# One rotation of three PSUM banks for the first product, the transposes and x, in place of one bank and a rotation of two

## The chip, the cores and the metric

The kernel runs on one core of one Trainium2 chip. The metric is the device time of one execution in microseconds (us), median of several runs. TensorE (PE in the rows), VectorE (DVE), ScalarE (ACT), GpSimd (POOL) and SyncE (SP, which issues the DMAs) each have a queue of their own that runs strictly in its order, and wait for each other through semaphores.

## The reference

Windowed attention with four sink tokens, then a gated MLP (the code calls it MoE; there is one expert). Batch 4, 8 heads, 768 positions, head size 64, window 128; the model is 512 wide, the hidden layer 1024. In short:

```python
scores = scale * np.matmul(q, k.transpose(0, 1, 3, 2))
scores = np.where(is_sink | in_window, scores, -1000000000.0)
a = softmax(scores)                         # in float32
x = np.matmul(a, v) .transpose(0, 2, 1, 3).reshape(B, S, H * D)
h = np.maximum(x @ w_in, 0.0)
conv_out[s] = sum(conv_w[k] * h[s + k - 1] for k in range(3))
gate = 1.0 / (1.0 + np.exp(-conv_out))
return h * gate @ w_out
```

## The kernel before

**Attention.** Heads are taken in pairs; pair `g` (0 to 15, four to a batch) has six query tiles of 128 rows, `t` = 0 to 5. `prep`/`prep32` turn q and k on TensorE (tiles `trq`, `trk` for batch 0, `tq`, `tk` after it), `scores` makes a tile of scores (`sc`, L330 in batch 0, L333 and L334 later), DVE takes the window and the maximum (L509, L510), ACT the exponential (L513), POOL scales by the sum (L518), `transp` turns the result (`pts`, L534 and L548), `transp_sinks` turns the sinks (`tk`, L541 and L568), and `pv` multiplies by v into `px` (L586, L609). `xout` copies `px` into the model's x, split into a high part `xH` (ACT, L341) and a low part `xL` (DVE, L342). For batch 0 `pv` works on half pairs, later on a whole pair, and then it holds two `px` tiles at once. Batch 0 is worked as pairs 0 to 3, first half, then pairs 0 to 3, second half.

**The MLP.** It is cut into 96 units: unit `n` has 256 positions and 128 hidden columns, 24 units to a batch. `first` makes the first product in 12 matmuls into `ph` (L184: each of four slices of the model takes three products, xH by wiH, xH by wiL, xL by wiH). `gate` reads `ph` once (ACT, L191), and then does the convolution and the gate: ACT L195, DVE L196 and L197, ACT L198, DVE L199, POOL L201 and L202, which write `g`. `second` multiplies `g` into `po` with six matmuls of 512 columns (L211). `pieces` lists these steps, the second product of a unit two units behind its first (`TRAIL` is 2), and `banded` hands them out between the steps of the attention at an even rate. A batch's units need the whole x of that batch, so units 24 to 47 come after `px` of pair 7; in batch 0 the `px` of pair 3's first half completes the first 384 positions, and units 0 to 7 (positions 0 to 255) can begin with them.

**The order.** The program text gives an order, but the Tile framework's scheduler then moves instructions: by its own estimate of times it puts on each engine's queue whatever it holds to be ready, within what data and buffers allow. `c.pin` does nothing in this version. A PSUM tile with a tag is put into the banks of that tag in turn, in the order of the program text: with `bufs=3`, a tile can't be written before the readers of the third one ahead of it are done. Eight banks are in use: `sc` 2, `pts` 1, `po` 2, and in the kernel before `h` 1 (the tiles `ph`) and `T` 2 (all turned tiles and `px`).

**Weights.** w_in and w_out come as 64-bit floats; `narrow` makes 32-bit ones on ACT (L112) and DVE (L113, L114, L115), and ACT and POOL split them (L122, L123). This goes on beside the attention of batch 0.

Of the kernel before, what the change touches and what calls it, by code (L numbers as in the profile page):

```python
# [10 lines left out]
F32 = mybir.dt.float32  # L11
F32R = mybir.dt.float32r
# [5 lines left out]
P = 128  # L18
# [43 lines left out]
class Moe:  # L62
# [62 lines left out]
    def taps(self, raw):  # L125
        c, nc = self.c, self.c.nc
        w = self.narrow(raw)
        pt = self.ps.tile([P, 512], F32, tag="T", name="cwt", bufs=2)
        c.pin(nc.tensor.transpose(pt[:, 0:3 * self.NFF], w, c.ident[0:3 * self.NFF, 0:3 * self.NFF]))
        nc.scalar.copy(self.cw.rearrange("p k f -> p (k f)"), pt[:, 0:3 * self.NFF])  # L130

# [31 lines left out]
    def unit(self, n):  # L163

        c, nc, mp = self.c, self.c.nc, self.mp
        NFF = self.NFF
        bc, ff = divmod(n, NFF)
        b, ch = divmod(bc, self.NCH)
        xH, xL = self.x(b)
        wH, wL = self.wi  # L170
        t0, t1 = max(0, CH * ch - 2), min(c.S, CH * ch + CH + 2)
        W = t1 - t0
        d0 = 1 if t1 < c.S else 3
        o = d0 - 1 + CH * ch - t0
        prods = [(w, x, cc) for cc in range(self.NCC) for (w, x) in ((wH, xH), (wL, xH), (wH, xL))]
        u = Ctx()

        def first(lo):
            if lo == 0:
                self.need(max(self.place[f"wi{ff * P // 512}_{self.NCC - 1}"], self.place["taps"]) + 1)  # L180
                u.h = self.ps.tile([P, 512], F32, tag="h", name=f"ph{n}")
            for i in range(lo, lo + 4):
                w, x, cc = prods[i]
                c.pin(nc.tensor.matmul(u.h[:, 0:W], w[:, cc, ff * P:(ff + 1) * P], x[:, cc, t0:t1],  # L184
                                       start=(i == 0), stop=(i == len(prods) - 1)))
            if lo + 4 == len(prods):
                gate()

        def gate():
            hb, cw = self.hb[n % 2], self.cw  # L190
            nc.scalar.activation(hb[:, d0:d0 + W], u.h[:, 0:W], AF.Relu, scale=0.5)  # L191
            prev, this, nxt = (hb[:, o + i:o + i + CH] for i in range(3))
            a = mp.tile([P, CH], F32, tag="t1", name=f"t1{n}")
            e = mp.tile([P, CH], F32, tag="t2", name=f"t2{n}")
            nc.scalar.mul(a, prev, cw[:, 0, ff:ff + 1])  # L195
            nc.vector.scalar_tensor_tensor(out=e, in0=this, scalar=cw[:, 1, ff:ff + 1], in1=a, op0=ALU.mult, op1=ALU.add)  # L196
            nc.vector.scalar_tensor_tensor(out=a, in0=nxt, scalar=cw[:, 2, ff:ff + 1], in1=e, op0=ALU.mult, op1=ALU.add)  # L197
            nc.scalar.activation(e, a, AF.Tanh)  # L198
            nc.vector.scalar_tensor_tensor(out=a, in0=e, scalar=1.0, in1=this, op0=ALU.add, op1=ALU.mult)  # L199
            u.g = mp.tile([P, 2, CH], F32R, tag="g", name=f"g{n}", bufs=NGB)  # L200
            nc.gpsimd.tensor_scalar(u.g[:, 0], a, 1.0, 1.0, ALU.mult, ALU.mult)  # L201
            nc.gpsimd.tensor_tensor(out=u.g[:, 1], in0=a, in1=f(u.g[:, 0]), op=ALU.subtract)  # L202

        def second(tt):
            self.need(self.place[f"wo{ff}"] + 1)
            if ff == 0:
                self.po[tt] = self.ps.tile([P, 512], F32, tag="po", name=f"po{n}{tt}", bufs=NT)
            po = self.po[tt]
            oH, oL = self.wo
            for i, (a, w) in enumerate(((0, oH), (0, oL), (1, oH))):  # L210
                c.pin(nc.tensor.matmul(po[:, 0:c.DM], u.g[:, a, tt * P:(tt + 1) * P], w[:, ff, :],  # L211
                                       start=(ff == 0 and i == 0), stop=(ff == NFF - 1 and i == 2)))
            if ff == NFF - 1:
                st = self.temp("st", c.DM, 3)
                nc.scalar.copy(st, po[:, 0:c.DM])
                nc.sync.dma_start(c.out[b, ch * CH + tt * P:ch * CH + (tt + 1) * P, :], st)

        u.first = [lambda lo=lo: first(lo) for lo in range(0, len(prods), 4)]
        u.second = [lambda tt=tt: second(tt) for tt in range(NT)]
        return u  # L220
# [15 lines left out]
class Attn:  # L236
# [15 lines left out]
    def prep(self, g, s, ahead=lambda: None):  # L252
# [4 lines left out]
        s.plain = False  # L257

        def turn_q(half):
            pt = self.mps.tile([P, HTL, P], F32, tag="T", name=f"tq{g}{half}", bufs=2)  # L260
            for t in range(HTL):
                c.pin(nc.tensor.transpose(pt[:, t, :], s.raw["q", half][:, t].rearrange("p a d -> p (a d)"), c.ident))  # L262
            ahead()
            X = s.X[half] = ap.tile([P, 2, HTL, P], F32R, tag="X", name=f"X{g}{half}", bufs=3)
            rows = [slice(D * j, D * j + D) for j in range(2)]
            for j in range(2):
                self.evac(X[rows[j], j], pt[rows[j]], -1.0 / math.sqrt(D))
            c.emptied = [nc.vector.scalar_tensor_tensor(out=X[rows[1 - j], j], in0=pt[rows[j]], scalar=-1.0 / math.sqrt(D),
                                                        in1=f(X[rows[j], j]), op0=ALU.mult, op1=ALU.subtract) for j in range(2)]

        def turn_k(half):
            if half == 0:
                if g % 2 not in self.KK:
                    self.KK[g % 2] = ap.tile([P, 4, T, kw], F32R, tag="kk", name=f"kk{g}")
                    for j in range(2):
                        r = slice(D - D * j, P - D * j)
                        plane = f(self.KK[g % 2][r, 2 + j]).rearrange("p t k -> p (t k)")
                        if self.zeros is None:
                            nc.gpsimd.memset(plane, 0.0)
                        else:  # L280
                            nc.sync.dma_start(plane, self.zeros[r])
                s.kk = self.KK[g % 2]
            kk = s.kk[:, :, HTL * half:HTL * half + HTL, 0:P]
            pt = self.mps.tile([P, HTL, P], F32, tag="T", name=f"tk{g}{half}", bufs=2)
            for t in range(HTL):
                c.pin(nc.tensor.transpose(pt[:, t, :], s.raw["k", half][:, t].rearrange("p a d -> p (a d)"), c.ident))
            ahead()
            for j in range(2):
                nc.scalar.copy(kk[:, j], pt)
            rows = [slice(D * j, D * j + D) for j in range(2)]  # L290
            c.emptied = [nc.vector.tensor_tensor(out=kk[r, 2 + j], in0=pt[r], in1=f(kk[r, j]), op=ALU.subtract)
                         for j, r in enumerate(rows)]
            if half == 0 and kw > P:
                nc.scalar.copy(s.kk[:, :, :, P:kw], f(s.kk[:, :, 0:1, 0:kw - P]).to_broadcast([P, 4, T, kw - P]))
            if half:
                nc.sync.dma_start(f(s.kk[D:P, 0]), f(s.kk[0:D, 0]))
                nc.sync.dma_start(f(s.kk[0:D, 1]), f(s.kk[D:P, 1]))
# [3 lines left out]
    def prep32(self, g, half, s, kk, tag, ahead):  # L301
# [2 lines left out]
        tiles = slice(HTL * half, HTL * half + HTL)  # L304

        def turn(nm):
            pt = self.mps.tile([P, HTL, P], F32, tag=tag, name=f"tr{nm}{g}{half}", bufs=2)
            for t in range(HTL):
                c.pin(nc.tensor.transpose(pt[:, t, :], s.raw[nm, half][:, t].rearrange("p a d -> p (a d)"), c.ident))
            if nm == "q":  # L310
# [79 lines left out]
def banded(c):  # L390
# [136 lines left out]
    def transp(g, t):  # L527
        s = st[g]
        hf, u = divmod(t, 3)
        if g < NPAIR:  # L530
# [4 lines left out]
            s.pT[t] = ap.tile([P, 2, 2, P], F32, tag="pT", name=f"pT{g}_{t}", bufs=PTB)  # L535
            nc.scalar.copy(s.pT[t][:, 0:parts], pts[:, 0:parts])  # L536
            if u == 2:
                pk = m.ps.tile([P, P], F32, tag="T", name=f"tk{g}_{t}", bufs=2)
                sk = ap.tile([P, 6, SP], F32, tag="sk", name=f"sk{g}_{hf}")
                nc.scalar.copy(sk, s.pe[hf].rearrange("p t h k -> p (t h) k")[:, :, P:P + SP])  # L540
                c.pin(nc.tensor.transpose(pk[0:6 * SP, :], sk.rearrange("p t k -> p (t k)"), c.ident))  # L541
# [20 lines left out]
    def transp_sinks(g, t):  # L562
        s = st[g]
        hf, u = divmod(t, 3)
        if g < NPAIR or u < 2:
            return
        pk = m.ps.tile([P, P], F32R, tag="T", name=f"tk{g}_{t}", bufs=2)
        c.pin(nc.tensor.transpose(pk[0:3 * SR, :], s.sk.rearrange("p a t k -> p (a t k)"), c.identr))  # L568
        s.sT[hf] = ap.tile([3 * SR, P], F32R, tag="sT", name=f"sT{g}_{hf}")
        s.cut.append(nc.scalar.copy(s.sT[hf], f(pk[0:3 * SR, :])))  # L570
# [1 line left out]
    def pv(g, t):  # L572
# [4 lines left out]
        if u < 2 or (g >= NPAIR and hf == 0):  # L577
            return
        halves = [hf] if g < NPAIR else [1, 0]
        px = {h: m.ps.tile([P, 3, P], F32, tag="T", name=f"px{g}_{h}", bufs=2).rearrange("p t k -> p (t k)") for h in halves}  # L580
        open_ = set()

        def product(j, kt, qt, pT):
# [30 lines left out]
    def prep(n):  # L614

        g, half = jobs[n]
        if g >= NPAIR and half:
            return []
        if g >= PLAIN:
            return A.prep(g, st[g], ahead)  # L620
        out = []
        for h in (half, half + 1)[0:1 + g // NPAIR]:
            out += A.prep32(g, h, st[g], kks[g // 2][:, g % 2], "po" if g < NPAIR and h == 0 else "T", ahead)
        return out

    def values(n):
# [83 lines left out]
def general(c):  # L710
# [12 lines left out]
    for g in range(c.B * NPAIR):  # L723
# [7 lines left out]
        for t in range(T):  # L731
            u = t % 3
            if u == 0:
                px = m.ps.tile([P, 3, P], F32, tag="T", name=f"px{g}_{t}", bufs=2)
            keep = gp.tile([P, S], F32, tag="keep", name=f"keep{g}_{t}", bufs=1)
            tmp = gp.tile([P, S], F32, tag="tmp", name=f"tmp{g}_{t}", bufs=1)
            wt = gp.tile([P, 1], F32, tag="wt", name=f"wt{g}_{t}", bufs=1)
# [112 lines left out]
```

## Time and profile before

| what | value |
|---|---|
| median of 3 runs | 501.5 us (501.25 to 502.39) |
| the profiled execution | 502.03 us |
| its span, first to last instruction | 499.9 us |
| TensorE busy | 458.4 us (92%) |
| VectorE, ScalarE, GpSimd busy | 359.9, 344.1, 287.6 us |
| mean granted TensorE clock | 0.98 of full speed |

The profiled execution's time is 2.13 us more than its span, and 0.53 us more than the median of the runs. A busy share is over the whole span; the rows below split it by stretch.

### The profile page before, as it was taken

What the parts mean: (1) busy time and instruction counts of PE and PEld (TensorE: products, weight loads), DVE (VectorE), ACT (ScalarE), POOL (GpSimd) and SP (SyncE); (2) the same over time, 40 slices, a digit from 0 to 9 for tenths busy, and PEclk for the clock granted to TensorE, in tenths of its full rate; (3) what the DMA queues carried; (4) which work ended last, traced back from release to release, by engine and by line L of the source; (5) the groups of instructions that cost most, each with busy time, mean ns of one, the idle gap of its engine ahead of it and who ended that gap; (6) DMA issues with size and microseconds to landing.
All of it is one profiled execution on the core that took longest, in us unless ns stands there. A gap on an engine that the chain in (4) does not pass through costs nothing.

```text
span 499.9 us, 10494 instructions
## 1 busy us (share of the span) xinstructions
PE 458.4 (92%) x3181; PEld 395.6 (79%) x3181; DVE 359.9 (72%) x1212; ACT 344.1 (69%) x1066; POOL 287.6 (58%) x558
## 2 busy tenths in 40 slices
PE   2878889998999999789999999999999999999993
PEld 1656678877888898578888898988888887889892
DVE  4677999767968787787876968596868663555561
ACT  3987897778858776685876777685967654444542
POOL 3457586643775656546674757475647673444441
PEclk9987899999999999899999999999999999999998
DMA  5875762246232423316241242143220100101101
GB/s 146 216 197 166 204 200 49 57 108 161 66 82 67 111 65 94 102 24 145 48 122 45 55 120 52 23 114 73 70 70 2 43 2 8 36 1 42 42 4 50
DMA packets 87307, 41.03 MB, mean 82 GB/s; under 512 B 80160, under 2 KB 80184, under 8 KB 87240
## 3 DMA queue, kind: packets, MB, share of 16 engines
q1 hardware_dynamic: 87240, 40.25, 30.9%
q8 instruction: 28, 0.46, 0.4%
q14 instruction: 39, 0.32, 0.2%
HBM read 27.60 MB, written 6.29 MB: 68 GB/s over the span
## 4 chain that ended last, share of the span: by engine, by line
PE 62%; DVE 14%; ACT 10%; POOL 5%; issue 3%; DMA 3%; SPq 2%; POOLq 0%; DVEq 0%; ACTq 0%
PE po L211 20%; PE ph L184 19%; PE px L586 7%; DVE t L197 3%; PE sc L333 3%; PE sc L334 3%; PE pts L548 3%; DVE t L196 2%; PE px L609 2%; PE sc L330 2%; ACT t L195 2%; ACT hb L191 2%; ACT t L198 1%; PE tq L262 1%; DVE stm L114 1%
## 5 line engine op out<-in xcount | busy, mean ns | idle before, releaser
L211 PE MATMUL po<-woH,g 128*128 128x512 f32 x384 | 139.4, 407 | 4.0 <-POOL g L201 3.9
L184 PE MATMUL ph<-xH,wiH 128*128 128x258 f32 (+1 forms) x384 | 111.9, 292 | 6.2 <-ACT hb L191 4.2
L184 PE MATMUL ph<-xL,wiH 128*128 128x258 f32 (+1 forms) x384 | 110.0, 286 | 0.4 <-DVE xL L342 0.4
L184 PE MATMUL ph<-xH,wiL 128*128 128x258 f32 (+1 forms) x384 | 108.9, 284 | 0.0
L201 POOL TENSOR_SCALAR g<-t 128x256 fp32r<-128x256 f32 x96 | 42.3, 441 | 75.2 <-DVE t L199 59.7
L211 PEld LDWEIGHTS po<-woH,g 128*128 128x128 f32 x384 | 70.0, 188 | 16.6 <-POOL g L201 5.7
L184 PEld LDWEIGHTS ph<-xH,wiH 128*128 128x128 f32 x384 | 72.7, 189 | 12.1 <-ACT hb L191 6.4
L202 POOL TENSOR_TENSOR g<-t,g 128x256 fp32r<-128x256 f32 x96 | 77.9, 812 | 5.4
L518 POOL TENSOR_SCALAR pe<-pe,sm 128x132 f32<-128x132 f32 (+1 forms) x144 | 62.3, 444 | 30.3 <-DVE sm L516 19.4
L211 PE MATMUL po<-woL,g 128*128 128x512 f32 x192 | 76.4, 398 | 0.0
L196 DVE SCALAR_TENSOR_TENSOR t<-hb,cw,t 128x256 f32<-128x256 f32 x96 | 51.2, 533 | 34.9 <-ACT t L195 34.7
L184 PEld LDWEIGHTS ph<-xH,wiL 128*128 128x128 f32 x384 | 72.7, 189 | 2.5
L184 PEld LDWEIGHTS ph<-xL,wiH 128*128 128x128 f32 x384 | 72.8, 190 | 1.9 <-DVE xL L342 1.4
L198 ACT ACTIVATE t<-t 128x256 f32<-128x256 f32 x96 | 40.1, 417 | 46.8 <-DVE t L197 46.4
L513 ACT ACTIVATE pe<-pe,sm 128x132 f32<-128x132 f32 (+1 forms) x144 | 58.0, 404 | 19.2 <-DVE sm L510 18.2
L199 DVE SCALAR_TENSOR_TENSOR t<-t,hb 128x256 f32<-128x256 f32 x96 | 45.4, 473 | 20.2 <-ACT t L198 19.5
L197 DVE SCALAR_TENSOR_TENSOR t<-hb,cw,t 128x256 f32<-128x256 f32 x96 | 54.8, 570 | 5.4
L195 ACT ACTIVATE t<-hb,cw 128x256 f32<-128x256 f32 x96 | 49.1, 511 | 5.6 <-POOL g L202 1.4
L191 ACT ACTIVATE hb<-ph 128x258 f32<-128x258 f32 (+1 forms) x96 | 36.9, 385 | 20.8 <-PE ph L184 20.2
L552 POOL TENSOR_SCALAR_AFFINE_SELECT pT<-pT 128x256 f32<-128x256 f32 x60 | 27.2, 454 | 40.1 <-ACT pT L550 32.4
L333 PE MATMUL sc<-kk,X 128*128 128x260 f32 (+1 forms) x144 | 44.1, 316 | 4.6 <-DVE sm L510 3.9
L586 PE MATMUL px<-pT,vraw 128*64 128x128 f32 (+1 forms) x512 | 44.6, 327 | 2.7 <-ACT pT L536 2.3
(145 smaller groups left out, 963.0 us busy)
## 6 DMA issues: line engine op xcount, KB each, us to landing
raw<-in_q_dram SPq DMA_DIRECT2D x64, 96.0 KB
raw<-in_k_dram SPq DMA_DIRECT2D x64, 96.0 KB
out_dram<-stm SPq DMA_DIRECT2D x24, 256.0 KB
kk<-kk SPq DMA_DIRECT2D x24, 198.0 KB
vraw<-in_v_dram SPq DMA_DIRECT2D x24, 192.0 KB
wi_0r<-in_moe_w_in_dram SPq DMA_DIRECT2D x2, 512.0 KB
wi_1r<-in_moe_w_in_dram SPq DMA_DIRECT2D x2, 512.0 KB
wi_2r<-in_moe_w_in_dram SPq DMA_DIRECT2D x2, 512.0 KB
```

The source lines that it names most:

```text
L184: c.pin(nc.tensor.matmul(u.h[:, 0:W], w[:, cc, ff * P:(ff + 1) * P], x[:, cc, t0:t1], start=(i == 0), stop=(i == len(prods) - 1)))
L191: nc.scalar.activation(hb[:, d0:d0 + W], u.h[:, 0:W], AF.Relu, scale=0.5)
L195: nc.scalar.mul(a, prev, cw[:, 0, ff:ff + 1])
L196: nc.vector.scalar_tensor_tensor(out=e, in0=this, scalar=cw[:, 1, ff:ff + 1], in1=a, op0=ALU.mult, op1=ALU.add)
L197: nc.vector.scalar_tensor_tensor(out=a, in0=nxt, scalar=cw[:, 2, ff:ff + 1], in1=e, op0=ALU.mult, op1=ALU.add)
L199: nc.vector.scalar_tensor_tensor(out=a, in0=e, scalar=1.0, in1=this, op0=ALU.add, op1=ALU.mult)
L202: nc.gpsimd.tensor_tensor(out=u.g[:, 1], in0=a, in1=f(u.g[:, 0]), op=ALU.subtract)
L211: c.pin(nc.tensor.matmul(po[:, 0:c.DM], u.g[:, a, tt * P:(tt + 1) * P], w[:, ff, :], start=(ff == 0 and i == 0), stop=(ff == NFF - 1 and i ...
L333: self.c.pin(self.nc.tensor.matmul(pc, X[:, j, u, :], kk[:, j, lo:hi], start=True, stop=False))
L513: nc.scalar.activation(pe[:, j, cols], pe[:, j, cols], AF.Exp, bias=sm[:, j:j + 1], scale=-1.0, accum_out=sm[:, 2 + 2 * j:3 + 2 * j])
L518: nc.gpsimd.tensor_scalar(pe[:, j, cols], pe[:, j, cols], sm[:, 8 + j:9 + j], 1.0, ALU.mult, ALU.mult)
L586: ins = nc.tensor.matmul(px[h][D * j:D * j + D, P * at:P * at + n], s.v[:, kt, j, :], pT, start=(h not in open_), stop=False, skip_group_c ...
```

## The change

The tiles `ph` and all tiles of the old tag `T` get one tag, `h`, with three buffers. The number of banks in use stays eight, and no instruction is added or taken away: each engine has the same work. What differs is the order in which tiles take a bank, and with it the order that the scheduler gives to every engine.

```diff
@@ taps, unit
-        pt = self.ps.tile([P, 512], F32, tag="T", name="cwt", bufs=2)
+        pt = self.ps.tile([P, 512], F32, tag="h", name="cwt", bufs=3)
...
-                u.h = self.ps.tile([P, 512], F32, tag="h", name=f"ph{n}")
+                u.h = self.ps.tile([P, 512], F32, tag="h", name=f"ph{n}", bufs=3)
@@ prep, prep32
-            pt = self.mps.tile([P, HTL, P], F32, tag="T", name=f"tq{g}{half}", bufs=2)
+            pt = self.mps.tile([P, HTL, P], F32, tag="h", name=f"tq{g}{half}", bufs=3)
...
-            pt = self.mps.tile([P, HTL, P], F32, tag=tag, name=f"tr{nm}{g}{half}", bufs=2)
+            pt = self.mps.tile([P, HTL, P], F32, tag=tag, name=f"tr{nm}{g}{half}", bufs=3 if tag == "h" else 2)
@@ banded: transp, transp_sinks, pv, prep
-                pk = m.ps.tile([P, P], F32, tag="T", name=f"tk{g}_{t}", bufs=2)
+                pk = m.ps.tile([P, P], F32, tag="h", name=f"tk{g}_{t}", bufs=3)
...
-        px = {h: m.ps.tile([P, 3, P], F32, tag="T", name=f"px{g}_{h}", bufs=2).rearrange("p t k -> p (t k)") for h in halves}
+        px = {h: m.ps.tile([P, 3, P], F32, tag="h", name=f"px{g}_{h}", bufs=3).rearrange("p t k -> p (t k)") for h in halves}
...
-            out += A.prep32(g, h, st[g], kks[g // 2][:, g % 2], "po" if g < NPAIR and h == 0 else "T", ahead)
+            out += A.prep32(g, h, st[g], kks[g // 2][:, g % 2], "po" if g < NPAIR and h == 0 else "h", ahead)
```

(Left out: the same edit for `tk` in `prep` and `transp_sinks`, and for `px` in `general`, the branch that these inputs don't take.)

TensorE's queue, pairs 7 and 8, just ahead of pair 7's `px`, in the kernel before. In a name the number behind the kind is the pair or the unit, then comes the query tile; the last number is a running one.

```order
L262 MATMUL tq81_2656<-ident_85,raw3_70 128x128 x3
L286 MATMUL tk90_2752<-ident_85,raw0_67 128x128 x3
L333 MATMUL sc8_0_0_2703<-kk4_1145,X80_2601 128x128
L334 MATMUL sc8_0_0_2703<-kk4_1145,X80_2601 128x128
L333 MATMUL sc8_0_1_2704<-kk4_1145,X80_2601 128x128
L334 MATMUL sc8_0_1_2704<-kk4_1145,X80_2601 128x128
L548 MATMUL pts_177<-ident_85,pe7_1_2560 128x128
L333 MATMUL sc8_1_0_2763<-kk4_1145,X80_2601 128x260
L334 MATMUL sc8_1_0_2763<-kk4_1145,X80_2601 128x260
L548 MATMUL pts_177<-ident_85,pe7_1_2560 128x128
L333 MATMUL sc8_1_1_2764<-kk4_1145,X80_2601 128x260
L334 MATMUL sc8_1_1_2764<-kk4_1145,X80_2601 128x260
```

The same place, from the scores of pair 8's first tile on, in the changed kernel:

```order
L211 MATMUL po160_2393<-woH_111,g20_2555 128x512
L211 MATMUL po160_2393<-woL_112,g20_2555 128x512
L211 MATMUL po161_2397<-woH_111,g20_2555 128x512
L211 MATMUL po161_2397<-woL_112,g20_2555 128x512
L333 MATMUL sc8_0_0_2703<-kk4_1145,X80_2601 128x128
L334 MATMUL sc8_0_0_2703<-kk4_1145,X80_2601 128x128
L548 MATMUL pts_177<-ident_85,pe7_1_2560 128x128 x2
L211 MATMUL po160_2393<-woH_111,g20_2555 128x512
L211 MATMUL po161_2397<-woH_111,g20_2555 128x512
L333 MATMUL sc8_0_1_2704<-kk4_1145,X80_2601 128x128
L334 MATMUL sc8_0_1_2704<-kk4_1145,X80_2601 128x128
L184 MATMUL ph23_2747<-xH0_116,wiH_109 128x258
```

In the kernel before no matmul of a unit stands between these scores; its next one, of unit 24, comes behind `px` of pair 7. In the changed kernel units 20 to 23 stand here. Counted over the whole queue, this many units' first products are complete ahead of each `px` (a fraction is a unit in work), and this many second products:

| ahead of `px` of pair | 4 | 5 | 6 | 7 | 8 | 9 | 11 | 15 |
|---|---|---|---|---|---|---|---|---|
| first products, before | 14 | 19 | 24 | 24.75 | 28 | 35 | 47 | 72 |
| first products, changed | 13 | 17 | 20 | 24 | 30 | 37 | 48 | 72 |
| second products, before | 11.67 | 16 | 21 | 24 | 26 | 32 | 44 | 69 |
| second products, changed | 10.67 | 15.67 | 19.67 | 23 | 28.67 | 35 | 47 | 70.67 |

TensorE's queue early in batch 0, in the kernel before, and then the same place in the changed kernel:

```order
L330 MATMUL sc2_2_1_513<-kks1_158,X20_322 128x260
L330 MATMUL sc3_0_0_541<-kks1_158,X30_446 128x128
L184 MATMUL ph0_736<-xH0_116,wiH_109 128x258
L184 MATMUL ph0_736<-xH0_116,wiL_110 128x258
L330 MATMUL sc3_0_1_542<-kks1_158,X30_446 128x128
L184 MATMUL ph0_736<-xL0_117,wiH_109 128x258
L330 MATMUL sc3_1_0_582<-kks1_158,X30_446 128x260
L534 MATMUL pts_177<-ident_85,roomL_119 128x128 x4
```

```order
L330 MATMUL sc2_2_1_513<-kks1_158,X20_322 128x260
L330 MATMUL sc3_0_0_541<-kks1_158,X30_446 128x128
L330 MATMUL sc3_0_1_542<-kks1_158,X30_446 128x128
L330 MATMUL sc3_1_0_582<-kks1_158,X30_446 128x260
L534 MATMUL pts_177<-ident_85,roomL_119 128x128 x4
```

Unit 0's matmuls stood one or two at a time between the attention's; now the first of them stands at this place, behind `px` of pair 3's first half:

```order
L586 MATMUL px3_0_721<-pT3_0_596,vraw1_72 64x128 x2
L609 MATMUL px3_0_721<-sT3_0_684,kks1_158 128x128 x2
L184 MATMUL ph0_736<-xH0_116,wiH_109 128x258
L184 MATMUL ph0_736<-xH0_116,wiL_110 128x258
L184 MATMUL ph0_736<-xL0_117,wiH_109 128x258
L184 MATMUL ph0_736<-xH0_116,wiH_109 128x258
L309 MATMUL trk11_741<-ident_85,raw3_70 128x128 x3
```

VectorE's queue when the scores of pair 0's fourth tile arrive (L510, `sc0_3`), in the kernel before, and then in the changed kernel; `stm` are the weights being narrowed, three instructions to a slice:

```order
L114 SCALAR_TENSOR_TENSOR stm21_624<-wi1_0r_580,stm21_624 128x512
L342 TENSOR_TENSOR xL0_117<-px2_0_598,xH0_116 128x384
L115 SCALAR_TENSOR_TENSOR stm21_624<-stm22_625,stm21_624 128x512
L510 ISA roomH_118,sm2_165<-sc0_3_0_662,roomH_118 128x260
L510 ISA sm2_165 128x1
L510 ISA roomH_118,sm2_165<-sc0_3_1_663,roomH_118 128x260
L510 ISA sm2_165 128x1
L113 TENSOR_SCALAR stm23_652<-stm24_653 128x512
L114 SCALAR_TENSOR_TENSOR stm23_652<-wi1_1r_632,stm23_652 128x512
```

```order
L114 SCALAR_TENSOR_TENSOR stm21_624<-wi1_0r_580,stm21_624 128x512
L115 SCALAR_TENSOR_TENSOR stm21_624<-stm22_625,stm21_624 128x512
L342 TENSOR_TENSOR xL0_117<-px2_0_598,xH0_116 128x384
L113 TENSOR_SCALAR stm23_652<-stm24_653 128x512
L114 SCALAR_TENSOR_TENSOR stm23_652<-wi1_1r_632,stm23_652 128x512
L115 SCALAR_TENSOR_TENSOR stm23_652<-stm24_653,stm23_652 128x512
L510 ISA roomH_118,sm2_165<-sc0_3_0_662,roomH_118 128x260
L510 ISA sm2_165 128x1
L510 ISA roomH_118,sm2_165<-sc0_3_1_663,roomH_118 128x260
```

The slice wi1_1 (L113, L114, L115) stood behind the two scores and now stands ahead of them.

## Rows read from the trace of the kernel before

**Rows 1.** Page, part 2: PE's busy tenths and granted clock, 40 slices.

```profile
PE   2878889998999999789999999999999999999993
PEclk9987899999999999899999999999999999999998
```

**Rows 2.** Windows from `px` to `px`, pairs 4 to 9: length, busy by engine, PEclk, DMA.

```profile
142.00:165.00 23.00, 22.52 (x169) 19.95 (x169) 16.87 (x69) 16.92 (x57) 14.30 (x31) 1.00 0.30 70
165.00:188.00 23.00, 23.00 (x174) 20.43 (x172) 18.06 (x68) 16.70 (x59) 13.89 (x32) 1.00 0.34 84
188.00:209.50 21.50, 17.73 (x118) 14.51 (x117) 16.65 (x75) 15.96 (x58) 13.30 (x31) 0.92 0.36 94
209.50:228.00 18.50, 16.79 (x126) 14.25 (x126) 14.35 (x56) 14.83 (x50) 10.32 (x23) 1.00 0.22 52
228.00:257.00 29.00, 28.51 (x208) 25.25 (x207) 22.75 (x86) 19.86 (x68) 19.19 (x39) 1.00 0.39 93
```

**Rows 3.** Timeline of PE, 196 to 222 us: its waits, in brackets with releaser.

```profile
203.86 0.56 PE L333 MATMUL sc<-kk,X 128*128 128x260 f32 x1 [2.86 <-DVE sm L510]
...
208.18 0.36 PE L333 MATMUL sc<-kk,X 128*128 128x260 f32 x1 [0.36 <-DVE sm L510]
...
209.53 2.60 PE L586 MATMUL px<-pT,vraw 128*64 128x128 f32 x28 [0.47 <-DVE kk L291]
...
215.97 0.41 PE L548 MATMUL pts<-ident,pe 128*128 128x128 f32 x2 [0.89 <-ACT pT L550]
```

**Rows 4.** Window behind the longest of these waits, columns as in rows 2.

```profile
204.00:208.00 4.00, 3.82 (x18) 3.25 (x18) 2.71 (x20) 3.18 (x15) 3.59 (x10) 0.60 0.00 0
```

**Rows 5.** Who PE waited for, whole span: us in total, times, longest.

```profile
PE ph L184 <- ACT hb L191: 4.2, 6, 1.1
PE po L211 <- POOL g L201: 3.9, 6, 1.5
```

**Rows 6.** Chain that ended last: a unit's second and first product, start and us.

```profile
436.70 1.42 PE po L211 x6
438.12 1.44 PE ph L184 x12
```

**Rows 7.** Windows of the first 80 us, columns as in rows 2.

```profile
20.00:40.00 20.00, 15.81 (x87) 11.96 (x85) 13.73 (x58) 17.56 (x60) 11.70 (x19) 0.83 0.72 201
40.00:60.00 20.00, 15.92 (x103) 12.43 (x103) 17.41 (x40) 15.27 (x40) 11.61 (x12) 0.83 0.70 193
60.00:80.00 20.00, 18.60 (x149) 16.03 (x146) 18.73 (x47) 17.49 (x50) 16.71 (x21) 1.00 0.61 170
```

**Rows 8.** Timeline of PE, 28 to 110 us: unit 0's first matmul, and a wait.

```profile
33.54 0.39 PE L184 MATMUL ph<-xH,wiH 128*128 128x258 f32 x1
...
52.70 0.39 PE L184 MATMUL ph<-xH,wiH 128*128 128x258 f32 x1 [1.86 <-ACT xH L341]
```

**Rows 9.** Timeline of DVE, 54 to 60 us: slice wi1_1's three instructions.

```profile
55.78 1.25 DVE L113 TENSOR_SCALAR stm<-stm 128x512 int32<-128x512 int32 x1
57.07 0.69 DVE L114 SCALAR_TENSOR_TENSOR stm<-wi_1r,stm 128x512 int32<-128x512 int32 x1
...
58.06 0.69 DVE L115 SCALAR_TENSOR_TENSOR stm<-stm,stm 128x512 int32<-128x512 int32 x1
```

**Rows 10.** Groups by line on ACT and DVE: readers of `ph` and `px`; busy us, mean ns, idle before.

```profile
L191 ACT ACTIVATE hb<-ph 128x258 f32<-128x258 f32 x64 | 24.5, 383 | 16.6 <-PE ph L184 16.2
...
L341 ACT CAST xH<-px 128x384 fp32r<-128x384 f32 x32 | 14.0, 478 | 8.8 <-PE px L609 8.8
...
L342 DVE TENSOR_TENSOR xL<-px,xH 128x384 fp32r<-128x384 f32 x32 | 17.0, 550 | 8.1 <-ACT xH L341 8.1
```

**Rows 11.** Windows of the tail, columns as in rows 2, and PE's last wait.

```profile
444.00:488.00 44.00, 44.00 (x283) 39.85 (x282) 26.14 (x47) 22.27 (x51) 21.34 (x31) 1.00 0.07 25
488.00:500.00 12.00, 4.36 (x18) 2.84 (x16) 2.12 (x4) 2.31 (x5) 2.28 (x4) 0.89 0.16 53
...
492.17 0.50 PE L211 MATMUL po<-woH,g 128*128 128x512 f32 x1 [1.48 <-POOL g L201]
```

More of the change, by code (lines that the diff above doesn't have):

```diff
@@ L283, in turn_k @@
             kk = s.kk[:, :, HTL * half:HTL * half + HTL, 0:P]
-            pt = self.mps.tile([P, HTL, P], F32, tag="T", name=f"tk{g}{half}", bufs=2)
+            pt = self.mps.tile([P, HTL, P], F32, tag="h", name=f"tk{g}{half}", bufs=3)
             for t in range(HTL):
@@ L566, in transp_sinks @@
             return
-        pk = m.ps.tile([P, P], F32R, tag="T", name=f"tk{g}_{t}", bufs=2)
+        pk = m.ps.tile([P, P], F32R, tag="h", name=f"tk{g}_{t}", bufs=3)
         c.pin(nc.tensor.transpose(pk[0:3 * SR, :], s.sk.rearrange("p a t k -> p (a t k)"), c.identr))
@@ L733, in general @@
             if u == 0:
-                px = m.ps.tile([P, 3, P], F32, tag="T", name=f"px{g}_{t}", bufs=2)
+                px = m.ps.tile([P, 3, P], F32, tag="h", name=f"px{g}_{t}", bufs=3)
             keep = gp.tile([P, S], F32, tag="keep", name=f"keep{g}_{t}", bufs=1)
```

## The prediction

> **What bounds the kernel now.** I read the page's slices first: TensorE is busy nine tenths or more in most of them, and the slices that are not are the first five or so, the one at four tenths of the way, and the last [rows 1]. So TensorE sets the time, and a change that gives it no less work can win only what it loses: idle time, and time at a clock below full. Its span of 499.9 us holds 41.5 us of idle. The windows say where. The first 60 us are thin (8.27 us idle in 20 to 60, at a granted clock of 0.83) [rows 7], the end is a chain (7.6 us idle) [rows 11], and between lies one odd place: from `px` of pair 6 to `px` of pair 7 TensorE is idle for 21.5 - 17.73 = 3.77 us and the clock is 0.92, and in the next window for 1.71 us, where the windows on both sides lose 0.48, 0 and 0.49 us [rows 2].
>
> The timeline of that place names the waits: 2.86 us for DVE's maximum, then 0.36, 0.47 and 0.89 us [rows 3], all by attention instructions that wait for attention on other engines. [...] The order shows why: the units of batch 0 had been drawn forward, all 24 first products were done ahead of `px` of pair 6, and those of batch 1 need `px` of pair 7. Nothing was left to fill with.
>
> The list of waits gives the direct cost of the single bank: TensorE waited six times, 4.2 us in all, for ACT to read the last `ph` [rows 5]. That is under 1% of the span, since the scheduler mostly put other work between two units.
>
> **The change, part by part.** No instruction is added, so every term is idle time won or lost. Prices of cover: a unit's first product is 12 matmuls in 1.44 us, 0.12 each, its second six in 1.42 us, 0.237 each [rows 6].
>
> *a. Batch 0's units are spread.* With a rotation in program order a unit cannot be drawn ahead of more than two other tiles of the tag, so units stay near where the program puts them. From `px` of pair 6 to that of pair 7 there were 9 first-product and 18 second-product matmuls; now there are 48 and 20: 39 x 0.12 + 2 x 0.237 = 5.2 us more cover at the place that lost 3.77 us plus 0.08 x 21.5 = 1.72 us of clock. To `px` of pair 8 there were 3.25 first and 2 second products, now 6 and 5.67, where 1.71 us were lost. Together the two windows lost 7.2 us [rows 2]. Bounds: 0 (the loss turns up elsewhere) to -7.2. The neighbours, with nine or more first and second products of units each, lose 0 to 0.5 us, so most should go; but there is one thinner place in the new order, ahead of `px` of pair 6: nine score tiles with only 16 second products (3.8 us) between. I take -5.5, nearer the full end, with 1.7 us left for that.
>
> *b. The bank of the first product.* The six waits of 4.2 us [rows 5] go where another bank is free. The reader of `ph` takes 0.38 us [rows 10]. Taking each matmul by its kind's price, before there were eight places where a unit's bank is written again with under 0.9 us of TensorE work since its last matmul (and six waits, 0.7 us each); in the new order four such places remain, two of them units. At 0.7 us three of these would cost 2.1. Bounds 0 to -4.2; I take -2.1. [...]
>
> *c. The start.* Unit 0's matmuls began at 33.54 us in gaps between attention [rows 8]; they now begin behind `px` of pair 3's first half. Until then TensorE idles a fifth of the time, so 12 x 0.12 = 1.44 us of work moves from gaps into a place where TensorE is 93% busy [rows 7]. The 1.86 us that TensorE stood before one of them for `xH` [rows 8] frees the matmuls behind it, but DVE was busy then with weights, so I count nothing for it. On DVE, slice wi1_1 (1.25 + 0.69 + 0.69 = 2.63 us) [rows 9] now stands ahead of two scores, and DVE is 94% busy between 60 and 80 us [rows 7], so attention falls behind by that much there. Summing the DVE queue by its rows' durations, the lag is 2.3 us at `px` of pair 0's second half and 0.5 at pair 1's, since the weights run out sooner. It costs only where TensorE has nothing else. Bounds 0 to 1.44 + 2.63 = +4.1; I take +1.5.
>
> *d. The rest.* In the tail TensorE is busy for all of 44 us [rows 11], and both orders end with the 18 second products of the last three units behind the last first product, so the last wait of 1.48 us [rows 11] and the chain of the gate stay: 0. Waits for `g` were 3.9 us in six places [rows 5], 1.5 of them in the last one; counted by the same prices, the TensorE work between a unit's first product and its second rises from 7.1 to 8.1 us at the median, which hides a little more, but I count 0 (bounds 0 to -1.5). The `px` pair holds two of three banks until ACT and DVE have copied both, 2 x 0.478 and 0.55 more [rows 10], about 1.5 us; behind every whole-pair `px` at least 2.9 us of TensorE work stands before one of these banks is written again. If that cover fails it is a rival, below.
>
> The sum: -5.5 - 2.1 + 1.5 = -6.1 us. The profiled execution took 502.03, so it would take 495.9; the median of the runs is 0.53 lower, so I give 495.4 for the median.
>
> **The rivals.**
>
> *Gain only at the banks.* The thin place moves to before `px` of pair 6 and loses there what it lost before pair 7: a is 0. For it: nine score tiles there against ten in the old thin place. Against: the 16 second products between them, and DVE at 16.65 of 21.5 us in the old place is not full [rows 2]. Time: 501.5 - 2.1 + 1.5 = 500.9.
>
> *Slower: `px` shuts the unit out.* Before, the unit's bank was its own; now the tile behind a `px` pair may have to wait for ACT and DVE, whose queues also hold gates and exponentials. For it: DVE already stood 8.1 us in all for `xH` ahead of `xL` [rows 10]. Against: the 2.9 us of cover. At 0.7 us (as for the old bank) at each of 12 whole pairs it costs 8.4 us: 495.4 + 8.4 = 503.8. It decides from 6.1 / 12 = 0.5 us a pair on.
>
> *Slower: the clock.* One wait of 2.86 us cost 1.6 us of clock behind it (4 x 0.40) [rows 3, 4], while stretches with waits under 0.7 us kept 1.00 [rows 2]. New waits of that length at each of the three batch ends, where units need a fresh x, would cost 3 x (2.86 + 1.6) = 13.4 us: 508.8. [...] In these rows short waits left the clock alone, so I give it little.
>
> *Nothing moves.* The order does change, as the lists show, but the terms may cancel: the start at its upper bound of +4.1, -2.1 at the banks, and a at -2: 501.5.
>
> **How the numbers follow.** Forecast 0.74 (491 to 500); gain only at the banks 0.10 (half of it below the bound, the rest within or just over); px 0.08; clock 0.02; nothing 0.06. A measurement of this kernel tells about 0.2%, 1 us, from no change, so below 500.5 is faster and above 502.5 slower: 0.79 faster, 0.09 same, 0.12 slower. The range: down to 491.0, a fully won (-7.2), the banks (-4.2) and the start at +1; up to 501.0, which takes in the banks' rival and leaves out about 0.15 above and 0.03 below.
>
> **What the changed profile would show.** Right on a: between `px` of pairs 5 and 8 no wait over 1 us, a granted clock of 1.00, and some 2 us idle per 40. Right on b: waits of L184 for ACT's `hb` under 2 us in all. Right on c: L184 first at some 60 us, more idle time between 30 and 60 than before, and `px` of pair 0's second half 0 to 3 us later than before. Right on d: the last 12 us as before. Wrong if 200 to 216 is full but as much idle time stands elsewhere, if `sc` waits for DVE ahead of `px` of pair 6, or if matmuls of L184, `tq` or `tk` wait for ACT's or DVE's copies of `px`.

## The result and the profile after

The changed kernel's median is 496.43 us (495.27 to 497.7) against 501.38 (501.25 to 502.39) for the kernel before beside it: 0.9897 of its time, interval 0.9868 to 0.9927. In a second comparison, experiment 7, it was 0.9884 (0.9865 to 0.9904). The forecast was 495.4 us, with a range of 491.0 to 501.0; the result lies 1.0 us above the one and inside the other. The profiled execution took 497.7 us, span 496.0.

First the page's slices, which answer to [rows 1]:

```profile
PE   2865888999999999999999999999999999999994
...
PEclk9987899999999999999999999999999999999999
```

The notch at four tenths of the span is gone, in both rows. The first slices are thinner than they were. The windows from `px` of pair 4 to `px` of pair 8, for [rows 2] (length, busy us and number by engine PE, PEld, DVE, ACT, POOL, granted clock, DMA share, GB/s):

```profile
142.60:164.15 21.55, 21.39 (x157) 18.55 (x159) 16.61 (x62) 15.61 (x54) 14.48 (x32) 1.00 0.34 81
164.15:187.15 23.00, 21.87 (x155) 18.11 (x157) 18.88 (x85) 18.34 (x67) 15.64 (x34) 1.00 0.33 82
187.15:207.30 20.15, 18.48 (x143) 16.11 (x143) 14.45 (x49) 14.59 (x48) 11.08 (x25) 1.00 0.35 82
207.30:234.80 27.50, 26.97 (x195) 23.75 (x197) 21.55 (x86) 20.62 (x69) 17.52 (x37) 1.00 0.35 88
```

From `px` of pair 5 to that of pair 8 TensorE is idle for 1.13 + 1.67 + 0.53 = 3.33 us and the clock stays at 1.00. Before it was 3.77 + 1.71 = 5.48 us idle, and 1.72 us of clock [rows 2]. The loss is spread thin and smaller by 3.9 us, not gone.

Who TensorE waited for, for [rows 5] (us in total, times, longest):

```profile
PE px L586 <- ACT pT L536: 4.3, 2, 2.5
...
PE pts L534 <- ACT pT L536: 3.6, 2, 2.9
PE po L211 <- POOL g L201: 3.0, 3, 1.7
...
PE ph L184 <- ACT sT L570: 0.9, 1, 0.9
...
PE ph L184 <- ACT hb L191: 0.2, 1, 0.2
```

The waits for the single bank went from 4.2 us in six times to 0.2 us in one. What is longer is the start: `pts` and `px` of batch 0 waiting for ACT's copies. Its windows, for [rows 7]:

```profile
20.00:40.00 20.00, 15.13 (x84) 11.27 (x82) 14.13 (x57) 17.51 (x60) 11.54 (x19) 0.83 0.73 202
40.00:60.00 20.00, 12.73 (x90) 9.94 (x89) 17.23 (x35) 14.84 (x37) 12.05 (x12) 0.82 0.68 195
60.00:80.00 20.00, 16.32 (x135) 14.04 (x136) 18.73 (x52) 17.10 (x49) 13.36 (x16) 1.00 0.61 171
```

TensorE idles for 4.87 + 7.27 + 3.68 = 15.8 us between 20 and 80, where it was 9.7 [rows 7]. So in these 60 us TensorE is busy for 6 us less, part of it because less work stands there, and the whole is still 5 us shorter.

**A ledger by stage.** Where TensorE stands at a `px` is not yet a gain or a loss, because by then it may have done more or fewer unit products. I counted them and priced half a unit (its first or its second product) at 1.43 us [rows 6]; the attention's matmuls ahead of these places are the same within two. To `px` of pair 3's second half the change is 1.45 us later with 1.75 halves less done, 1.75 x 1.43 = 2.50: a loss of 3.95. At `px` of pair 8 it is 6.55 us later, but 4.67 halves ahead (6.68): the stage between won 4.1. At `px` of pair 15 it is 0.07 later and 1.67 halves ahead (2.39): another 2.2. The rest of the span won 1.6, and 3.9 us is the difference of the two spans.

The idle time alone tells another story. TensorE was busy for 458.4 of 499.9 us before and for 454.5 of 496.0 us now, so it was idle for 41.5 us in both. Up to `px` of pair 3's second half the idle time rose from 22.6 to 28.4 us, from there to `px` of pair 8 it fell from 8.4 to 5.3, and behind that from 10.6 to 7.7. What is shorter is the busy time. Some 2.1 us of it are clock, as an estimate from its mean (499.9 x 0.020 before, 496.0 x 0.016 now). Another 1.4 us lie in the first 36 unit matmuls, which stood partly alone in gaps before and now stand together (L184 up to `px` of pair 0's second half, before and now):

```profile
0.00:71.97 71.97, 7.24 (x36) 5.17 (x36) 0.91 0.69 188
...
0.00:74.53 74.53, 5.81 (x36) 4.79 (x36) 0.91 0.66 183
```

The tail, for [rows 11], windows and the last wait:

```profile
440.00:484.00 44.00, 44.00 (x275) 39.58 (x274) 24.28 (x48) 21.29 (x50) 19.85 (x32) 1.00 0.07 25
484.00:496.00 12.00, 4.84 (x21) 3.28 (x19) 2.15 (x4) 2.51 (x6) 2.27 (x4) 0.92 0.16 52
...
488.36 0.51 PE L211 MATMUL po<-woH,g 128*128 128x512 f32 x1 [1.19 <-POOL g L201]
```

It is as it was.

### The profile page after: what moved, and what is told of

It reads as the page before. It is cut to its first block, busy times and chain, and to the rows that moved or that the text cites. A ratio compares the mean times of both kernels' runs of the same rounds, so it can differ in the third digit from the quotient of the medians.

```text
span 496.0 us, 10528 instructions
## 1 busy us (share of the span) xinstructions
PE 454.5 (92%) x3181; PEld 392.7 (79%) x3181; DVE 355.5 (72%) x1212; ACT 343.8 (69%) x1066; POOL 285.5 (58%) x558
## 4 chain that ended last, share of the span: by engine, by line
PE 65%; DVE 16%; POOL 6%; ACT 6%; issue 3%; DMA 2%; SPq 1%; POOLq 0%; ACTq 0%; DVEq 0%
PE po L211 22%; PE ph L184 22%; PE px L586 7%; PE sc L333 3%; PE sc L334 2%; PE px L609 2%; PE pts L548 2%; DVE X L268 2%; DVE t L197 2%; DVE t L196 2%; PE sc L330 2%; DVE stm L114 2%; DVE kk L291 1%; DVE sc L509 1%; DVE pe L510 1%
## 5 line engine op out<-in xcount | busy, mean ns | idle before, releaser
L184 PE MATMUL ph<-xH,wiH 128*128 128x258 f32 (+1 forms) x384 | 112.0, 292 | 1.6 <-ACT sT L570 0.9
L184 PE MATMUL ph<-xH,wiL 128*128 128x258 f32 (+1 forms) x384 | 109.2, 285 | 0.0
L184 PE MATMUL ph<-xL,wiH 128*128 128x258 f32 (+1 forms) x384 | 108.4, 284 | 0.0
L201 POOL TENSOR_SCALAR g<-t 128x256 fp32r<-128x256 f32 x96 | 42.8, 446 | 84.9 <-DVE t L199 60.6
L211 PEld LDWEIGHTS po<-woH,g 128*128 128x128 f32 x384 | 68.7, 188 | 16.0 <-POOL g L201 5.4
L518 POOL TENSOR_SCALAR pe<-pe,sm 128x132 f32<-128x132 f32 (+1 forms) x144 | 63.2, 450 | 31.1 <-DVE sm L516 14.4
L202 POOL TENSOR_TENSOR g<-t,g 128x256 fp32r<-128x256 f32 x96 | 73.8, 770 | 5.8
L184 PEld LDWEIGHTS ph<-xH,wiH 128*128 128x128 f32 x384 | 72.7, 189 | 5.0 <-ACT sT L570 1.3
L196 DVE SCALAR_TENSOR_TENSOR t<-hb,cw,t 128x256 f32<-128x256 f32 x96 | 51.7, 540 | 31.6 <-ACT t L195 31.1
L184 PEld LDWEIGHTS ph<-xH,wiL 128*128 128x128 f32 x384 | 72.7, 189 | 2.1
L184 PEld LDWEIGHTS ph<-xL,wiH 128*128 128x128 f32 x384 | 72.5, 189 | 1.0
L195 ACT ACTIVATE t<-hb,cw 128x256 f32<-128x256 f32 x96 | 49.0, 513 | 11.3 <-POOL g L202 8.8
L197 DVE SCALAR_TENSOR_TENSOR t<-hb,cw,t 128x256 f32<-128x256 f32 x96 | 49.9, 520 | 4.1 <-POOL pe L518 0.5
L586 PEld LDWEIGHTS px<-pT,vraw 128*64 128x64 f32 x512 | 32.1, 143 | 16.6 <-ACT pT L536 5.0
L509 DVE COPY_PREDICATED sc<-before,sc 128x128 f32<-128x128 int32 x120 | 33.1, 291 | 16.3 <-PE sc L334 15.3
```

The costliest lines, as they stand in the source:

```text
L518: nc.gpsimd.tensor_scalar(pe[:, j, cols], pe[:, j, cols], sm[:, 8 + j:9 + j], 1.0, ALU.mult, ALU.mult)
L586: ins = nc.tensor.matmul(px[h][D * j:D * j + D, P * at:P * at + n], s.v[:, kt, j, :], pT, start=(h not in open_), stop=False, skip_group_c ...
```

## The experiments

Two theories stood against each other. *Spread*: the time comes from the order, since a shared rotation keeps batch 0's units from being drawn forward (term a). *Banks*: it comes from the two further banks that a first product may use (term b). The kernels were compared with the kernel before on their own chip, whose median was 501.93 us beside the first four and 502.33 beside the last three.

**1. The spread order without the banks.** The kernel before, with its one bank and two. An ordering on TensorE's queue alone, with no semaphore, keeps the first matmul of units 8 to 23 behind the last scores that stand ahead of it in the program text.

```diff
+TIED = range(8, 24)
...
-                c.pin(nc.tensor.matmul(u.h[:, 0:W], w[:, cc, ff * P:(ff + 1) * P], x[:, cc, t0:t1],
-                                       start=(i == 0), stop=(i == len(prods) - 1)))
+                ins = nc.tensor.matmul(u.h[:, 0:W], w[:, cc, ff * P:(ff + 1) * P], x[:, cc, t0:t1],
+                                       start=(i == 0), stop=(i == len(prods) - 1))
+                if i == 0 and n in TIED and c.marks:
+                    c.tc.add_manual_dep(ins.ins, c.marks[-1].ins.name, mybir.DependencyInfo(
+                        mybir.DependencyClass.NoSync, mybir.DependencyReason.DATA), reason="tie")
```

> The kernel before, with its own bank for the unit and two for the rest, and nothing but an order added on TensorE: the first matmul of each of units 8 to 23 may not stand ahead of the last scores emitted before it. No bank changes. Ahead of pair 7's x there are then 21 units at pair 6's x, not 24. If spreading batch 0's units is what gains (the spread theory), this kernel gains 3 to 6 us against the kernel before, some 496 to 498 us, with the start of the kernel before and without the loss that the changed kernel shows there. If the gain comes from the further banks for the first product (the bank theory), it stays within 1 us of the kernel before, 501.4.

Measured: 496.19 us (495.24 to 497.62), 0.9883 (0.9854 to 0.9913). That is a gain as large as that of the change, with none of its banks. Its windows around the old notch, and its two longest waits of units (lines in this kernel are a few further down: L185 is the first product, L195 the copy to `hb`):

```profile
200.00:220.00 20.00, 18.05 (x137) 15.09 (x136) 15.41 (x66) 16.19 (x56) 12.51 (x29) 1.00 0.19 45
220.00:240.00 20.00, 20.00 (x147) 17.29 (x146) 15.49 (x54) 12.60 (x41) 13.30 (x28) 1.00 0.52 127
...
PE ph L185 <- ACT hb L195: 5.5, 7, 1.3
PE po L215 <- POOL g L205: 3.4, 7, 1.0
```

The 20 us from 200 lose 1.95 at a clock of 1.00, where the kernel before lost 4.61 there at a clock of 0.91:

```profile
200.00:220.00 20.00, 15.39 (x110) 12.77 (x110) 14.43 (x66) 15.01 (x56) 10.78 (x29) 0.91 0.30 77
```

The waits for the bank even rose, from 4.2 to 5.5 us. By the ledger this kernel loses nothing to `px` of pair 3's second half, wins 4.3 us from there to `px` of pair 8, and 0.7 behind it, where it waits in the same places as the kernel before. So term a is real and needs no bank.

**2. The banks without the spread order.** The changed kernel, where the planner hands units 8 to 23 out over 17 steps in place of 25, so that they stand early again: at `px` of pair 6 all 24 first products are done, as before.

```diff
-    cuts = {NSTB // 2: (0, 1, NSTB // 2), NSTB: (1, m.NCH, NSTB + 1)}
+    cuts = {NSTB // 2: (0, 1, NSTB // 2), NSTB: (1, m.NCH, 17)}
```

> The changed kernel with its rotation of three, and batch 0's units handed out over 17 steps in place of 25, so that all 24 are done ahead of pair 6's x again, as in the kernel before. The spread theory expects 3 to 7 us to be lost against the changed kernel, 499 to 503 us, with waits and a lower clock again between pair 6's x and pair 7's. The bank theory expects no change against the changed kernel, 496.4 within 1 us.

Measured: 502.11 us (499.77 to 503.98), 1.0002 (0.9979 to 1.0024): all of the gain is gone, with three banks in rotation. The windows show the old notch again, and its clock:

```profile
200.00:220.00 20.00, 16.29 (x108) 13.54 (x109) 13.96 (x74) 13.94 (x56) 10.63 (x29) 0.83 0.34 91
220.00:240.00 20.00, 17.92 (x136) 15.59 (x135) 17.04 (x60) 16.16 (x54) 12.05 (x24) 1.00 0.32 74
```

3.71 and 2.08 us idle, the first at a clock of 0.83. By the ledger against the kernel before, the start lost 3.0 us and the stretch from there to `px` of pair 8 another 1.9, and the rest of the span won 4.3: what the rotation won behind batch 0 was eaten by both. The time is close to that of the rival "gain only at the banks", whose sum gave 500.9.

**3. The rotation with two banks.** The changed kernel, every `bufs=3` of the shared tag made 2.

```diff
-                u.h = self.ps.tile([P, 512], F32, tag="h", name=f"ph{n}", bufs=3)
+                u.h = self.ps.tile([P, 512], F32, tag="h", name=f"ph{n}", bufs=2)
```

> The changed kernel with two banks in the rotation in place of three, so one PSUM bank lies idle and every tile of the rotation has fewer banks than in the kernel before. The order of the units stays spread (20 at pair 6's x). The spread theory expects most of the gain to stay: faster than the kernel before by 1 to 4 us, 497.5 to 500.5, slower than the changed kernel by the waits for two banks. The bank theory expects it to be slower than the kernel before, over 502.4.

Measured: 512.8 us (512.18 to 513.92), 1.0222 (1.0184 to 1.0259). The spread theory expected a gain here and got a loss: this run refutes it as an account of what the number of banks is worth. The list of waits (L568's `tk` tile of the sinks is what `sT` is copied from), and windows from 100 us on:

```profile
PE tq L262 <- ACT sT L570: 3.8, 3, 1.6
PE ph L184 <- ACT sT L570: 3.3, 4, 1.1
...
PE sc L333 <- DVE X L268: 2.5, 2, 1.3
...
100.00:160.00 60.00, 55.04 (x417) 47.92 (x416) 46.11 (x175) 46.33 (x151) 31.11 (x70) 1.00 0.38 93
160.00:200.00 40.00, 36.21 (x269) 30.56 (x268) 31.27 (x124) 30.32 (x104) 22.98 (x54) 1.00 0.36 89
200.00:240.00 40.00, 37.77 (x262) 32.73 (x261) 31.38 (x126) 29.61 (x101) 24.85 (x53) 1.00 0.28 68
240.00:400.00 160.00, 153.86 (x1105) 134.69 (x1104) 119.76 (x427) 113.72 (x366) 95.57 (x202) 1.00 0.27 68
```

TensorE loses 4.96 + 3.79 + 2.23 + 6.14 = 17.1 us from 100 to 400, where the changed kernel loses 6.7. It is a little nearly everywhere. The largest cause that the list names is 7.1 us in seven waits, since a unit or a turned q may not be written until ACT has read the tile of the sinks two places ahead. With three banks that releaser is down to one wait of 0.9 us. So the third bank doesn't win time against the kernel before; it keeps the shared rotation from costing some 16 us.

**4. ACT's order at the start.** In the changed kernel ACT's copy of pair 2's third turned scores stands behind the narrowing of a weight slice, and TensorE waits 2.50 us for it (49.72 on its timeline); before it stood ahead. The edit puts the ninth slice's L112 behind the last such copy, again by order alone.

```diff
-        nc.scalar.mul(low, f(hi), 2.0 ** -112)
+        ins = nc.scalar.mul(low, f(hi), 2.0 ** -112)
+        if self.c.copies and self.done == 8:
+            self.c.tc.add_manual_dep(ins.ins, self.c.copies[-1].ins.name, mybir.DependencyInfo(
+                mybir.DependencyClass.NoSync, mybir.DependencyReason.DATA), reason="tie")
```

> The changed kernel with one order added on ACT: narrowing slice wo3 (L112) may not stand ahead of the last copy of pair 2's turned scores (L536), behind which it stood in the kernel before. In the changed kernel that copy waited behind L112, which waited for GpSimd, and pair 2's px came 3 us later. If this is what the start lost, the kernel gains about 2 us on the changed one, 494.4; if the start lost it by unit 0's matmuls being moved out of gaps, or by VectorE's order, nothing changes, 496.4 within 1 us.

Measured: 499.14 us (497.51 to 499.6), 0.9941 (0.9918 to 0.9964). Neither 494.4 nor 496.4 came: it is slower than the changed kernel in experiment 7, while its interval just overlaps that of the first comparison (up to 0.9927). The edit did what it should, since `px` of pair 2 now begins at 46.30 us after a wait of 0.68, but the idea failed. The start's windows:

```profile
40.00:60.00 20.00, 14.16 (x74) 10.28 (x74) 16.72 (x34) 15.12 (x39) 12.70 (x12) 0.74 0.68 198
60.00:80.00 20.00, 16.98 (x135) 15.14 (x132) 16.42 (x49) 16.99 (x47) 15.81 (x18) 0.91 0.53 148
```

TensorE is idle for less of the time (5.84 and 3.02 us), but at a clock of 0.74 and 0.91. The busy time that was won holds no more matmuls: 74 in 14.16 us and 135 in 16.98, where the changed kernel's windows above have 90 in 12.73 and 135 in 16.32. This one profile was the quickest of its executions, so where the others lose their time stays open.

**5. The old start, then the rotation.** One bank and two until batch 0's attention ends, then three in rotation: if the start's loss counted in the end, this would win it back.

```diff
+    def bank(self, kind, shape, dtype, name):
+        if self.apart:
+            return self.rot.tile(shape, dtype, tag=kind, name=name, bufs=1 if kind == "h" else 2)
+        return self.rot.tile(shape, dtype, tag="h", name=name, bufs=3)
...
-                u.h = self.ps.tile([P, 512], F32, tag="h", name=f"ph{n}", bufs=3)
+                u.h = self.bank("h", [P, 512], F32, f"ph{n}")
...
+    SWITCH = NSTB
```

> Both in turn: up to the end of batch 0's attention the banks are those of the kernel before (one for the unit, two for the rest), and behind it the rotation of three of the changed kernel. The queues then begin as in the kernel before and go on spread as in the changed one. If the start cost the changed kernel some 4 us, the spread gained some 4 to 5 and the further banks some 3 to 4, each apart from the others, this kernel takes all gains without the loss: 492 to 493.5 us, faster than the changed kernel by 3 to 4. If the start's loss was given back later in the changed kernel anyway, or the gains are one and the same, it stays within 1 us of the changed kernel.

Measured: 496.65 us (494.88 to 498.03), 0.9882 (0.9856 to 0.9907), the same as the changed kernel. The start was indeed restored: `px` of pair 3's second half began at 115.37 us with 16 halves of units done, where the changed kernel had 15 at 116.73: 1.36 + 1.43 = 2.8 us ahead. At `px` of pair 8 less than a microsecond of that was left. Where it went (this kernel's window, and some of its waits, L351 being the scores, L201 the first product):

```profile
100.00:160.00 60.00, 54.31 (x405) 46.61 (x403) 45.08 (x175) 45.36 (x151) 33.43 (x71) 1.00 0.41 99
...
119.07 0.36 PE L351 MATMUL sc<-kk,X 128*128 128x260 f32 x1 [0.68 <-DVE sm L529]
...
132.84 0.39 PE L351 MATMUL sc<-kk,X 128*128 128x260 f32 x1 [0.70 <-DVE sm L529]
...
PE sc L351 <- DVE sm L529: 3.6, 7, 0.7
...
PE ph L201 <- ACT hb L208: 2.3, 2, 1.3
```

and the changed kernel's in the same stretch:

```profile
100.00:160.00 60.00, 57.10 (x422) 49.24 (x421) 46.71 (x178) 47.07 (x154) 33.63 (x73) 1.00 0.39 97
```

5.69 us idle against 2.90. Of this, 1.3 us are a wait for the single bank at 105.31, still ahead of pair 3's `px`. From that `px` to the one of pair 8 this kernel is idle for 7.2 us and the changed one for 5.3, which is 1.9 of the 2.0 us that were lost. All seven waits of scores for DVE's maxima (3.6 us) lie there; in the changed kernel the scores wait for L510 there once, for 0.2 us. The likely reason, which no run shows by itself: the units are handed out at an even rate by the program text, so a TensorE that arrives early has nothing more to fill with.

**6. Units 0 to 7 behind the scores.** The kernel before with the ordering of experiment 1, but for units 0 to 7, so that unit 0 leaves the gaps of the start. Its first matmul then ran at 55.85 us, not at 33.54 as before, nor at 62.35 as in the changed kernel.

```diff
-TIED = range(8, 24)
+TIED = range(0, 8)
```

> The kernel before with its banks, and only units 0 to 7 tied: none may begin ahead of the last scores emitted before it, so that unit 0's matmuls leave the gaps of the first 60 us, as in the changed kernel, while ACT's queue stays as in the kernel before to 60 us. If moving unit 0 out of the gaps is what the start lost, px of pair 3's second half comes 1 to 3 us later than 115.3 with the same or less work done, and the time is 502.5 to 504.5; if the loss hangs on ACT's order, it comes at 115.3 and the time stays within 1 us of the kernel before. Batch 0's units are packed as before or more, so the loss ahead of pair 7's x should be there in either case.

Measured: 504.1 us (501.06 to 506.17), 1.0041 (1.0019 to 1.0063). The time is as expected, the place is not: `px` of pair 3's second half began at 115.07, not later than before (115.28), with the same work done. But in this execution the clock from 20 to 40 us was 0.91 and not 0.83, worth 20 x 0.08 = 1.6 us, so by an estimate the move cost 1.4 us there, as c had it. And a part of the loss lies where the ordering did not touch anything (idle 2.34 us here; in the kernel before 0.66 or less in any 20 us from 240 to 440):

```profile
320.00:340.00 20.00, 17.66 (x114) 15.98 (x114) 15.81 (x61) 15.96 (x53) 12.74 (x29) 0.91 0.39 98
```

So a small edit at the start shifts the scheduler's order much later too, and the 2 us can't be put down to unit 0 alone.

**7. The changed kernel again**, unedited, for its profile.

> The changed kernel itself once more, beside the others on one chip: 0.990 of the kernel before, as in its first timing, if that ratio holds from chip to chip (within 0.003).

Measured: 496.34 us (495.64 to 496.92), 0.9884 (0.9865 to 0.9904). This profiled execution took 495.88, span 494.2, 1.8 less than the first. The start, answering to the windows above:

```profile
20.00:40.00 20.00, 15.72 (x108) 12.27 (x107) 15.28 (x62) 18.40 (x62) 11.91 (x20) 0.91 0.74 206
40.00:60.00 20.00, 12.85 (x89) 9.62 (x87) 17.62 (x34) 15.14 (x38) 12.29 (x12) 0.83 0.71 204
60.00:80.00 20.00, 16.32 (x129) 14.43 (x128) 17.43 (x50) 16.94 (x47) 14.70 (x18) 1.00 0.59 157
```

From 20 to 40 us TensorE is busy 0.59 us more, at a clock of 0.91 in place of 0.83. At `px` of pair 0's second half this execution is 1.87 us ahead (72.66 against 74.53), at pair 8's 2.0, at the end 1.8; behind the start the two go alike. By the ledger this execution had lost 1.8 us at `px` of pair 3's second half, not 3.95.

## Why the prediction was right, and where not

**a, the spread (-5.5).** Shown. The order alone gives 0.9883, or 496.19 - 501.93 = -5.7 us, and with the order undone three banks give 1.0002. The signs asked for are there: no wait over 0.92 us between `px` of pairs 5 and 8, a clock of 1.00, and 3.33 us idle in 70.65, or 1.9 in 40. By the ledger the place itself won 4.1 us in the changed kernel and 4.3 in experiment 1, of the 7.2 that were lost there, so -5.5 was some 1.3 us too much. One sign of being wrong did show, "as much idle time stands elsewhere": the sum over the span is 41.5 us in both profiles (40.3 in experiment 7's). The working took every term for "idle time won or lost". Between the two profiles idle time only moved to the start, and what was won over the whole span is clock and busy time.

**b, the bank (-2.1).** The waits fell from 4.2 to 0.2 us, below the 2 us asked for. Its size is not shown. By the ledger the stretch from `px` of pair 8 to the end won 3.8 us in the changed kernel and 4.3 in experiment 2, whatever batch 0's order; in experiment 1, whose units have one bank, it won 0.7. But the waits of that stretch, in the kernel before and then in the changed one, are not for the bank alone:

```profile
PE po L211 <- POOL g L201: 2.8, 4, 1.5
PE ph L184 <- ACT hb L191: 1.3, 3, 0.5
...
PE po L211 <- POOL g L201: 1.2, 1, 1.2
```

1.3 us of waits for the bank went, and 1.6 of waits for `g`, which the prediction had under d. Whether the later batches' order or the further bank took these away was not tested. The runs show that rotation with the old order gains nothing in the total, and that the order without rotation gains as much as the change.

**c, the start (+1.5).** This is the term that was mis-sized most. The step that failed is the lag "2.3 us at `px` of pair 0's second half and 0.5 at pair 1's, since the weights run out sooner". At pair 0's it was 2.56, as summed; at pair 1's 6.70 (92.94 against 86.24), and by the ledger 3.95 us were lost in the end, near the bound of 4.1; in experiment 7's execution 4.9 and 1.8. I summed DVE's queue, while the loss went round through ACT: copies of `pT` came late (waits of 2.92, 2.50 and 1.84 us for L536, where the kernel before waited 1.77, 0.17 and 0.31 us for `px`), which no term held. L184 first ran at 62.35 us, as foretold. How the 3.95 us split between unit 0 (1.4 by the estimate of experiment 6), DVE's slice wi1_1 and ACT's order stays open: no run moved the slice alone, and the one on ACT's order made things worse.

**The sum.** -5.5 - 2.1 + 1.5 = -6.1 was foretold, and -5.0 and -6.0 us were measured in the two comparisons. That it came so close is partly luck. By the ledger of the first profile the start is +3.95 where +1.5 was foretold, the place -4.1 in place of -5.5, and all behind `px` of pair 8 -3.8, where only part of b's -2.1 and nothing of d was expected: the errors cancel. Nor do the terms add. Experiment 5 takes c away and keeps a and b, and gains nothing: what the start saves is lost again until pair 8.

**d, the rest (0).** The last wait is 1.19 us against 1.48 [rows 11], and the last 12 us hold 0.48 us less idle time: right within half a microsecond. Not so the waits for `g`, which d left at 0: the three between `px` of pairs 8 and 15, 1.3 us, are gone.

**The rivals.** *Gain only at the banks*: refuted for this change. Experiment 2, where only the order of batch 0 differs, comes near its time, with a loss at the start and the place that is larger than the rival had. *`px` shuts the unit out*: in the changed kernel no matmul of L184, `tq` or `tk` waits for a copy of `px`. A turned q of batch 0 (`trq`) waits for one, `xL`, for 0.7 us, and a unit for `sT` for 0.9 us, once each. Experiment 3 shows that the mechanism exists and where it sets in: a tile in the rotation that is held shuts out what follows, at two banks for 7.1 us in seven waits for `sT` alone. *The clock*: 1.00 in every 20 us from 60 to 480. In the other runs with three banks (experiments 2, 4, 5 and 7) it is 1.00 in every 20 us from 80 to 480, but for 0.83 in the notch of experiment 2, where units had run out as in the kernel before.

No version beat the changed kernel: the spread by order alone and the old start with the rotation behind it are equal to it within their intervals. But they are not equal in their parts: experiment 1 wins at the place and loses nothing at the start, while in the changed kernel the place pays for the start and what is left is won behind `px` of pair 8.

## What to carry to other kernels

When tiles of several kinds share a rotation of banks, ask first what that does to the order: the rotation follows the program text, and a scheduler that had drawn filler work forward no longer may. Here that was worth 4 us, and an ordering without a new bank gave as much as the whole change. The number of banks decided the sign here: with three the change won 1%, with two it cost 2.2%. And don't add up terms of different stages where filler is handed out at a fixed rate: a start that was 2.8 us quicker kept 0.8 of it four pairs later, with 1.9 us more idle time between.

## What was not expected of the chip

Two executions of one kernel differ in the start by their granted clock, 0.83 against 0.91 from 20 to 40 us, and the whole difference of 1.8 us between their spans is there at 47 us: on the chain that ended last in both, a pair of POOL's L518 begins at 45.63 in the one and at 43.81 in the other, and POOL's L123 behind it at 46.84 and 44.96. TensorE is busy for about three quarters of that stretch in both (15.13 and 15.72 of 20 us). Of a gain of 1% on this kernel, a single profile can thus show a third too much or too little; the ledger by stage needs the clock of each stage beside it.
